# A Linformer attention and SwiGLU kernel: the second batch turned by DMA, k' turned over 128 rows, and the first batch's v' laid out by TensorE

## The chip, the cores and the metric

One core of a Trainium2 chip runs the whole program. The metric is the device time of one execution in microseconds. Before the change the median of 8 runs was 573.11 us (572.68 to 574.63).

A core has TensorE (matmuls, into PSUM), VectorE (DVE), ScalarE (ACT), GpSimd (POOL) and SyncE (SP), each with its own queue of instructions that runs in the order in which the program lists them; they wait for each other through semaphores. DMA transfers are issued from POOL (all loads that change float32 to bf16), from SP (stores and turns) and from ACT.

## The reference

There are 8 batches of 8 heads, 1024 tokens and 64 elements a head. E and F project the 1024 tokens of k and v to 64 rows, so that attention is over 64 columns. The result is the input of a gated feed-forward block.

```python
k_proj = np.einsum('ks,bhsd->bhkd', E, k)
v_proj = np.einsum('ks,bhsd->bhkd', F, v)
scores = scale * np.matmul(q, k_proj.transpose(0, 1, 3, 2))
attn = softmax(scores)                       # over 64 columns
x = np.matmul(attn, v_proj)                  # -> [8192, 512]
g = x @ w_gate                               # [8192, 1536]
out = (g * sigmoid(g) * (x @ w_val)) @ w_out # [8192, 512]
```

## The kernel before, in words

**Tiles.** A batch's 1024 tokens make two tiles of 512 (`ch` 0 and 1), so the feed-forward block runs over 16 tiles `c = 2 b + ch`. In each, 12 column blocks `f` of 128 are worked off. `f_g` makes four matmuls of 512 columns into a `gps` bank and has ACT take the tanh; `f_v` makes four into a `vps` bank and has DVE multiply twice, into `hT`. The product with `w_out` of the tile before (`f_y`, parts of four matmuls into a `yps` bank, three parts to one of the four output blocks) is dealt out between them; for the first tile it begins only at the fifth block of the second (`ypart`), and there a block carries one or two parts.

**The attention's units.** For each batch: `u_KV` projects k and v (matmuls with 64 stationary columns: k to PSUM rows 0 to 63, v to rows 64 to 127), copies k' to a tile `ks` of 64 rows and v' into the block-diagonal `BDV`. `u_KT` turns k' with four TensorE transposes, one a pair of heads, into a bf16 PSUM tile, and four DVE copies bring it into the block-diagonal `BD`. Queries must stand with their elements on the partitions: either `u_T` turns four 128x128 blocks of them on TensorE and copies them out of PSUM, or `u_TD` has one DMA on the SP queue turn the 512 tokens of a tile, from `qb` to `qTd`. `u_S` makes four score matmuls and the exponential on ACT, `u_R` sums and takes the reciprocal on DVE, `u_N` multiplies on POOL. The softmax weights must be turned again: `u_A` on TensorE with a copy, or `u_AD` by one DMA on SP. `u_PV` multiplies by v' and copies into `xT`, the feed-forward block's input. A tile has four units of T, S, R, N and A and four of PV. `BY_DMA` says which tiles take the DMA way: all of batches 1 to 7 but the first tile of batch 1.

**The order.** The schedule is written by hand (`manual_schedule`): each engine's queue has the order of the program's text. The feed-forward loop has 192 steps `t`, `t = 12 c + f`; slot `2t` comes after `f_g`, slot `2t + 1` after `f_v` and the step's `f_y` parts. `put(slot, unit, ...)` hangs an attention unit into a slot, `place(b)` does so for batch b. In a slot loads go first, the rest in the order of the `put` calls. So TensorE runs through `f_g`, a slot's units, `f_v`, `f_y`, a slot's units; a unit whose input isn't there stops all that follows.

**The start.** Ahead of the loop batch 0's first tile is worked off unit by unit. Its loads, then the weights in pairs of column blocks (`load_w_gv`), the second tile's queries, `wo` and batch 1's k are issued on POOL, in text order, mixed with the `u_N` there; `warm` gives TensorE matmuls on zeros. In the first two steps the tile's two halves of 256 tokens are made apart (`u_PV2`, `f_mm` with `i`). Batch 0's second tile hangs in slots 12 to 23, batch 1 in slots 30 to 69.

**Buffers that matter.** Three PSUM banks `pa` for the attention, two `gps`, two `vps`, one `yps`; four `qb`, two each of `kb`, `vb`, `qTd`, `AT`, `AAd` and `xT` of each half; three `ysb` for outputs.

Of the kernel before, what the change touches and what calls it, by code (L numbers as in the profile page):

```python
# [15 lines left out]
B = 8  # L16
H = 8
# [13 lines left out]
BY_DMA = [(b, ch) for b in range(1, B) for ch in range(CH)][1:]  # L31
# [3 lines left out]
def kernel(  # L35
# [39 lines left out]
    BDV = [const.tile([P, NPAIR, P], BF16, name=f"BDV{i}") for i in range(2)]  # L75
    ET = const.tile([P, NJ, KP], BF16, name="ET")
# [26 lines left out]
    def load_q(b, ch, js=(0, 4)):  # L103
        if js[0] == 0:
            qb[b, ch] = q_pool.tile([P, H, 4, D], BF16, name="qb", tag="qb")
        js = slice(*js)
        nc.gpsimd.dma_start(  # L107
            out=qb[b, ch][:, :, js, :].rearrange("p h j d -> p h (j d)"),
            in_=q[b].rearrange("h (p c j) d -> p c h j d", c=2, j=4)[:, ch, :, js, :].rearrange(
                "p h j d -> p h (j d)"  # L110
            ),
        )
# [26 lines left out]
    def u_KV(b, what="kv", hs=(0, H), at="a"):  # L139

        key = (b, what)
        if key not in kvp:
            kvp[key] = bank(at, [P, H, D], FP32, "kvp")
        t = kvp[key]
        h0, h1 = hs
        todo = [x for x in (("k", 0, ET, kb), ("v", 64, FT, vb)) if x[0] in what]
        for j in range(NJ):
            for _, lo, w, src in todo:
                nc.tensor.matmul(  # L149
                    out=t[lo : lo + 64, h0:h1].rearrange("p h d -> p (h d)"),  # L150
                    lhsT=w[:, j, :],
                    rhs=src[b][:, h0:h1, j, :],
                    start=(j == 0),
                    stop=(j == NJ - 1),
                )
        if "k" in what:
            if (b, "s") not in kvp:
                kvp[b, "s"] = aw.tile([KP, H, D], BF16, name="ks", tag="ks")
            nc.scalar.copy(out=kvp[b, "s"][:, h0:h1], in_=t[0:64, h0:h1])  # L159
        if "v" in what:  # L160
            tv = t[64:128].rearrange("p (a c) d -> p a c d", c=2)
            ps = slice(h0 // 2, h1 // 2)
            eng = nc.vector if b else nc.scalar
            copy(eng, BDV[b % 2][0:64, ps, 0:64], tv[:, ps, 0, :])
            copy(eng, BDV[b % 2][64:128, ps, 64:128], tv[:, ps, 1, :])
        if h1 == H:
            kvp.pop(key)

    def u_KT(b, at="a", prs=(0, NPAIR)):

        ks = kvp[b, "s"]
        t = bank(at, [P, NPAIR, KP], BF16, "kTp")
        for pr in range(*prs):
            nc.tensor.transpose(
                out=t[:, pr, :],
                in_=ks[:, 2 * pr : 2 * pr + 2, :].rearrange("p h d -> p (h d)"),
                identity=ident_bf[:KP, :KP],
# [132 lines left out]


# [80 lines left out]
    def place(b):  # L392
        s0 = 48 * (b - 1)
        if b == 1:
            put(30, u_TD, 1, 1)
            put(34, u_KV, 1, "k")
            put(36, u_KT, 1)
            put(40, u_KV, 1, "v")
            sa = (37, 38, 39, 40, 48, 50, 52, 54)
            tt = (35, 36, 37, 38)  # L400
            ta = (41, 42, 43, 44)
            put(57, u_AD, 1, 1)
            sp = (43, 44, 45, 46, 66, 67, 68, 69)
        else:
            put(s0, u_KV, b)
            put(s0 + 3, u_KT, b)
            o = 14 if b == 2 else 6
            put(s0 + (3 if b == 2 else -6), u_TD, b, 0)
            put(s0 + (5 if b == 2 else -4), u_TD, b, 1)
# [4 lines left out]
        for j in range(NJ):  # L414
            if (b, j // 4) not in BY_DMA:
                put(tt[j], u_T, b, j)
                put(ta[j], u_A, b, j)
# [10 lines left out]
    with tc.manual_schedule():  # L428
# [17 lines left out]
        for i in range(2):  # L446
            nc.vector.memset(BD[i][:], 0.0)
            nc.vector.memset(BDV[i][:], 0.0)

# [65 lines left out]
        u_R(0, 3)  # L515
        u_N(0, 3)
        u_KV(0, "v", (0, 4), at="y")
        warm(1)
        u_KV(0, "v", (4, 6), at="y")
        u_PV2(0, 0, 0, 0, act)  # L520
        u_A(0, 2, dve)
        u_KV(0, "v", (6, 8), at="y")
        u_A(0, 1, act)
        u_PV2(0, 0, 1, 0, act)
        u_A(0, 3, dve)
        u_PV2(0, 0, 0, 1, dve)
        load_w_gv(4, 6)
        load_q(0, 1)
        for f in (6, 8, 10):
            load_w_gv(f, f + 2)  # L530
        load_wo(0)
        load_wo(1)
        load_k(1)
        f_mm(0, 0, 0, 0)
        u_PV2(0, 0, 1, 1, act)
        f_mm(0, 0, 1, 0)
        f_mm(0, 1, 0, 0)
        f_mm(0, 1, 1, 0)

        for i, u in enumerate(range(4, 8)):  # L540
            put(12 + i, u_T, 0, u)
            put(14 + i, u_S, 0, u)
            put(15 + i, u_R, 0, u)
            put(15 + i, u_N, 0, u)
            put(19 + i, u_A, 0, u, nc.scalar)
        put(21, u_PV, 0, 1, 0)
        put(22, u_PV, 0, 1, 1)
        put(23, u_PV, 0, 1, 2)
        put(23, u_PV, 0, 1, 3)
        put(20, load_q, 1, 0)  # L550
# [4 lines left out]
        for b in range(2, B):  # L555
            s0 = 48 * (b - 1) - (12 if b == 2 else 24)
            put(s0, load_k, b)
            put(s0 + 2, load_v, b)
            put(s0 + 4, load_q, b, 0)
            put(s0 + 6, load_q, b, 1)  # L560
# [53 lines left out]
```

The softmax here doesn't subtract the row's maximum and nothing guards it: scores larger than these inputs give would overflow.

## Time and profile before

| | |
|---|---|
| median of 8 runs | 573.11 us |
| the profiled execution's own time | 573.3 us |
| its span | 571.5 us |
| TensorE busy | 564.8 us |
| VectorE, ScalarE, GpSimd busy | 336.7, 238.3, 109.3 us |
| read from HBM, written | 60.29 MB, 16.78 MB |

The span runs from the program's first instruction to its last. A line of the timeline gives start and length in us, engine, line of the program, operation, what is written from what, shapes and how many instructions were merged; in brackets, idle time ahead and what ended it. A matmul's length is from its issue to its last result, so successive ones overlap: what TensorE really spends on a group is the distance from its start to the next group's start. Some matmul records are missing.

### The profile page before, as it was taken

The page shows a single profiled execution, that of the slowest core. Times are in us where ns is not written, and L with a number is a line of the kernel's source. Part 1 is how long each engine was busy: PE and PEld are TensorE (multiplying, and loading weights), DVE is VectorE, ACT ScalarE, POOL GpSimd, SP SyncE. Part 2 cuts the span into 40 slices and gives each one's busy share as a digit, 9 for nine tenths or more (in the row PEclk, how much of TensorE's full clock was granted, in tenths as well). Part 3 has the DMA queues.
Part 4 walks back from the last instruction along what each step waited for, and adds up shares of the span by engine and source line. Part 5 has one row for each costly group of instructions (what it writes and reads, how often), then busy time and mean ns, then how long its engine had stood idle before and what let it go on. Part 6 is the DMA issues. An engine that isn't in the chain of part 4 may idle for free.

```text
span 571.5 us, 7944 instructions
## 1 busy us (share of the span) xinstructions
PE 564.8 (99%) x2971; PEld 268.7 (47%) x2971; DVE 336.7 (59%) x581; ACT 238.3 (42%) x421; POOL 109.3 (19%) x122
## 2 busy tenths in 40 slices
PE   8999999999999999999999999999999999999997
PEld 4654444444444444444444444444444444444444
DVE  3777566666466654666556664567546674554540
ACT  3555534354435434444335434354342543443232
POOL 6734122134002500124001330023200220000000
PEclk9999999999999999999999999999999999999999
DMA  9999993549901697038950499204990123100012
GB/s 209 171 200 206 202 174 79 87 74 195 203 27 48 114 192 145 19 75 131 189 106 37 65 174 193 67 20 93 194 175 36 44 50 75 38 37 24 33 38 92
DMA packets 106983, 61.86 MB, mean 108 GB/s; under 512 B 60096, under 2 KB 98240, under 8 KB 106944
## 3 DMA queue, kind: packets, MB, share of 16 engines
q0 software_dynamic: 42800, 29.36, 35.7%
q1 hardware_dynamic: 63232, 30.42, 24.8%
q10 hardware_dynamic: 912, 1.57, 0.9%
q8 instruction: 23, 0.38, 0.3%
q14 instruction: 16, 0.13, 0.1%
HBM read 60.29 MB, written 16.78 MB: 135 GB/s over the span
## 4 chain that ended last, share of the span: by engine, by line
PE 92%; DMA 3%; POOL 1%; DVE 1%; ACT 1%; issue 0%; DVEq 0%; POOLq 0%
PE yps L362 29%; PE vps L324 28%; PE gps L324 27%; PE kvp L149 3%; PE sc L229 2%; PE pv L287 2%; DMA wv<-in_moe_w_val_dram 2%; DMA kb<-in_k_dram 2%; DVE zz L244 1%; POOL wg L117 0%; DVE hT L348 0%; ACT xT L137 0%; POOL qb L107 0%; DVE s L343 0%; POOL AA L260 0%
## 5 line engine op out<-in xcount | busy, mean ns | idle before, releaser
L343 DVE SCALAR_TENSOR_TENSOR s<-th,gps 128x512 f32<-128x512 f32 x192 | 130.6, 680 | 139.1 <-ACT th L336 138.7
L324 PE MATMUL gps<-xT,wg 128*128 128x512 bf16 (+1 forms) x776 | 197.8, 377 | 0.6 <-DMA wg<-in_moe_w_gate_dram 0.4
L324 PE MATMUL vps<-xT,wv 128*128 128x512 bf16 (+1 forms) x776 | 197.5, 377 | 0.1
L362 PE MATMUL yps<-wo,hT 128*128 128x512 bf16 (+1 forms) x780 | 194.5, 376 | 0.0
L336 ACT ACTIVATE th<-gps 128x512 f32<-128x512 f32 x192 | 114.6, 597 | 163.4 <-PE gps L324 161.9
L348 DVE TENSOR_TENSOR hT<-s,vps 128x512 bf16<-128x512 f32 x192 | 132.0, 688 | 22.1 <-PE vps L324 1.5
L362 PEld LDWEIGHTS <-hT 128*128 128x128 bf16 x780 | 76.1, 98 | 89.9
L260 POOL TENSOR_TENSOR AAd<-ee,rr 128x512 bf16<-128x512 f32 x52 | 54.1, 1040 | 319.5 <-issue 178.1
L324 PEld LDWEIGHTS <-wv 128*128 128x128 bf16 x776 | 73.8, 98 | 83.1 <-issue 3.3
L324 PEld LDWEIGHTS <-wg 128*128 128x128 bf16 x776 | 74.0, 98 | 81.8 <-DMA wg<-in_moe_w_gate_dram 0.9
L372 ACT ACTIVATE ysb<-yps 128x512 f32<-128x512 f32 (+1 forms) x65 | 38.4, 590 | 78.1 <-PE yps L362 78.1
L137 ACT CAST xT<-pv 128x512 bf16<-128x512 f32 x63 | 36.7, 584 | 51.2 <-PE pv L287 50.3
L244 DVE TENSOR_REDUCE zz<-ee 128x8 f32<-128x512 f32 x64 | 43.4, 679 | 19.4 <-ACT ee L233 19.3
L233 ACT ACTIVATE ee<-sc 128x512 f32<-128x512 f32 x64 | 37.9, 596 | 17.8 <-PE sc L229 17.7
L287 PE MATMUL pv<-AT,BDV 128*128 128x512 bf16 x60 | 22.6, 379 | 0.0
L229 PEld LDWEIGHTS <-qTd 128*128 128x128 bf16 x208 | 16.0, 98 | 12.3
L229 PE MATMUL sc<-BD,qTd 128*128 128x128 bf16 x208 | 20.1, 219 | 0.0
L137 DVE CAST BDV<-kvp 64x256 bf16<-64x256 f32 x14 | 6.0, 427 | 22.1 <-ACT ks L159 19.1
L260 POOL TENSOR_TENSOR AA<-ee,rr 128x512 bf16<-128x512 f32 x11 | 11.4, 1038 | 36.3 <-DVE rr L246 34.4
L246 DVE RECIPROCAL rr<-zz 128x8 f32<-128x8 f32 x64 | 13.0, 203 | 6.7 <-DVE zz L244 0.5
L149 PE MATMUL kvp<-kb,ET 128*64 128x512 bf16 (+1 forms) x72 | 15.5, 357 | 0.6 <-DMA kb<-in_k_dram 0.4
L149 PE MATMUL kvp<-vb,FT 128*64 128x512 bf16 (+2 forms) x80 | 15.6, 338 | 0.3 <-ACT BDV L137 0.3
(51 smaller groups left out, 147.4 us busy)
## 6 DMA issues: line engine op xcount, KB each, us to landing
out_dram<-ysb SPq DMA_DIRECT2D x63, 256.0 KB, 2.4
qb<-in_q_dram POOLq DMA_DIRECT2D x15, 512.0 KB, 16.8
kb<-in_k_dram POOLq DMA_DIRECT2D x7, 1024.0 KB, 11.3
vb<-in_v_dram POOLq DMA_DIRECT2D x7, 1024.0 KB, 14.4
wo<-in_moe_w_out_dram POOLq DMA_DIRECT2D x2, 768.0 KB, 15.3
wg<-in_moe_w_gate_dram POOLq DMA_DIRECT2D x5, 256.0 KB, 9.6
wv<-in_moe_w_val_dram POOLq DMA_DIRECT2D x5, 256.0 KB, 10.2
kraw<-in_k_dram ACTq DMA_DIRECT2D x2, 512.0 KB, 5.1
```

The lines of the kernel that those rows point to most:

```text
L137: (nc.scalar.copy if eng is nc.scalar else eng.tensor_copy)(out=out, in_=in_)
L149: nc.tensor.matmul(out=t[lo : lo + 64, h0:h1].rearrange("p h d -> p (h d)"), lhsT=w[:, j, :], rhs=src[b][:, h0:h1, j, :], start=(j == 0), ...
L229: nc.tensor.matmul(out=ps[:, n, :], lhsT=t[:, n, :], rhs=BD[b % 2][:, 4 * g + n, :], start=True, stop=True)
L233: nc.scalar.activation(out=e[:].rearrange("p h j k -> p (h j k)"), in_=ps[:].rearrange("p a k -> p (a k)"), func=AF.Exp, scale=scale,)
L244: nc.vector.reduce_sum(out=z[:], in_=e[:], axis=AX.X)
L260: eng.tensor_tensor(out=a.rearrange("p j h k -> p h j k"), in0=ee.pop((b, u))[:], in1=rr.pop((b, u))[:].unsqueeze(3).to_broadcast([P, 4, 2 ...
L324: nc.tensor.matmul(out=ps[:, ts], lhsT=(wg, wv)[w][:, kt, f * P : (f + 1) * P], rhs=x[:, kt, ts], start=(kt == 0), stop=(kt == NKT - 1),)
L336: nc.scalar.activation(out=th[:], in_=ps[:], func=AF.Tanh, scale=0.5)
L343: nc.vector.scalar_tensor_tensor(out=s1[:], in0=th[:], scalar=1.0, in1=g[:], op0=ALU.add, op1=ALU.mult)
L348: nc.vector.tensor_tensor(out=hT[c][:, f, :], in0=s1[:], in1=ps[:], op=ALU.mult)
L362: nc.tensor.matmul(out=yy[c][:, cs], lhsT=hT[c][:, f, i * P : (i + 1) * P], rhs=wo[:, f, cs], start=(f == 0), stop=(f == NFT - 1),)
L372: nc.scalar.activation(out=ysb[:, cs], in_=yy[c][:, cs], func=AF.Copy, scale=0.5)
```

## The change

- `BY_DMA` takes in batch 1's first tile: its `u_T` and `u_A` are gone, a `u_TD` (slot 22) and a `u_AD` (slot 41) come. Batch 1's other units move: k in slot 29, k' turned in 32, scores in 35 to 38 and 41 to 44, `u_AD` of the second tile in 47.
- k' is kept in two constant tiles `ks` of 128 rows whose lower half is zero, and `u_KT` uses ordinary matmuls over all 128 rows into a float32 PSUM tile.
- Batch 0's v' is made by a new `u_V0` that writes the block-diagonal form in PSUM (a matmul on zeros first, then v in two column halves), so that one copy on ACT brings it to `BDV`. It is split over pairs 0 and 1, pair 2, pair 3, with a new `u_PV1` for one pair; the units around it and the first `f_mm` are put in another order.
- Loads: the queries of batch 0's second tile in two halves by heads, between the weights; batch 1's first queries and k ahead of `wo`; batch 2's k, v and queries in slots 43 to 45 (before, in 36 to 42), batch 3's four slots later than before.
- Batch 0's second tile moves one slot ahead, its `u_A` to 17, 18, 20, 21, its `u_PV` to 19, 20, 22, 22, the last with its copy on DVE. In batch 2 k and v are projected in slot 56 (before 48), k' turned in 59, `u_TD` in 57 and 59, and the scores start in 61 (before 62).

```diff
...
 NIT = B * CH * NFT
-BY_DMA = [(b, ch) for b in range(1, B) for ch in range(CH)][1:]
+BY_DMA = [(b, ch) for b in range(1, B) for ch in range(CH)]
 @with_exitstack
...
     BDV = [const.tile([P, NPAIR, P], BF16, name=f"BDV{i}") for i in range(2)]
+    ks = [const.tile([P, H, D], BF16, name=f"ks{i}") for i in range(2)]
     ET = const.tile([P, NJ, KP], BF16, name="ET")
...
             )
-    def load_q(b, ch, js=(0, 4)):
-        if js[0] == 0:
+    def load_q(b, ch, js=(0, 4), hs=(0, H)):
+        if js[0] == 0 and hs[0] == 0:
             qb[b, ch] = q_pool.tile([P, H, 4, D], BF16, name="qb", tag="qb")
-        js = slice(*js)
+        js, hs = slice(*js), slice(*hs)
         nc.gpsimd.dma_start(
-            out=qb[b, ch][:, :, js, :].rearrange("p h j d -> p h (j d)"),
-            in_=q[b].rearrange("h (p c j) d -> p c h j d", c=2, j=4)[:, ch, :, js, :].rearrange(
+            out=qb[b, ch][:, hs, js, :].rearrange("p h j d -> p h (j d)"),
+            in_=q[b, hs].rearrange("h (p c j) d -> p c h j d", c=2, j=4)[:, ch, :, js, :].rearrange(
                 "p h j d -> p h (j d)"
...
         if "k" in what:
-            if (b, "s") not in kvp:
-                kvp[b, "s"] = aw.tile([KP, H, D], BF16, name="ks", tag="ks")
-            nc.scalar.copy(out=kvp[b, "s"][:, h0:h1], in_=t[0:64, h0:h1])
+            nc.scalar.copy(out=ks[b % 2][0:64, h0:h1], in_=t[0:64, h0:h1])
         if "v" in what:
...
             ps = slice(h0 // 2, h1 // 2)
-            eng = nc.vector if b else nc.scalar
-            copy(eng, BDV[b % 2][0:64, ps, 0:64], tv[:, ps, 0, :])
-            copy(eng, BDV[b % 2][64:128, ps, 64:128], tv[:, ps, 1, :])
+            nc.vector.tensor_copy(out=BDV[b % 2][0:64, ps, 0:64], in_=tv[:, ps, 0, :])
+            nc.vector.tensor_copy(out=BDV[b % 2][64:128, ps, 64:128], in_=tv[:, ps, 1, :])
         if h1 == H:
             kvp.pop(key)
+    def u_V0(p0, p1, at):
+        t = bank(at, [P, p1 - p0, P], FP32, "kvp")
+        nc.tensor.matmul(
+            out=t[:].rearrange("p a d -> p (a d)"),
+            lhsT=zeros[:, 0:P], rhs=zeros[:, 0 : (p1 - p0) * P],
+            start=True, stop=False,
+        )
+        src = vb[0][:].rearrange("p (a c) j d -> p a c j d", c=2)
+        for j in range(NJ):
+            for c in range(2):
+                nc.tensor.matmul(
+                    out=t[64 * c : 64 * c + 64, :, 64 * c : 64 * c + 64],
+                    lhsT=FT[:, j, :],
+                    rhs=src[:, p0:p1, c, j, :],
+                    start=False,
+                    stop=(j == NJ - 1),
+                )
+        nc.scalar.copy(out=BDV[0][:, p0:p1, :], in_=t[:])
     def u_KT(b, at="a", prs=(0, NPAIR)):
-        ks = kvp[b, "s"]
-        t = bank(at, [P, NPAIR, KP], BF16, "kTp")
+        t = bank(at, [P, NPAIR, KP], FP32, "kTp")
         for pr in range(*prs):
-            nc.tensor.transpose(
+            nc.tensor.matmul(
                 out=t[:, pr, :],
-                in_=ks[:, 2 * pr : 2 * pr + 2, :].rearrange("p h d -> p (h d)"),
-                identity=ident_bf[:KP, :KP],
+                lhsT=ks[b % 2][:, 2 * pr : 2 * pr + 2, :].rearrange("p h d -> p (h d)"),
+                rhs=ident_bf[:, 0:KP],
+                start=True,
+                stop=True,
             )
...
         copy(eng, xT[b, ch][:, 2 * g : 2 * g + 2, 256 * i : 256 * (i + 1)], ps[:])
+    def u_PV1(b, ch, pr, i, eng):
+        ps = ps_a.tile([P, CW // 2], FP32, name="pv", tag="pa")
+        nc.tensor.matmul(
+            out=ps[:].rearrange("p (j t) -> p j t", t=P),
+            lhsT=BDV[b % 2][:, pr, :],
+            rhs=AT[b, ch][:, 2 * i : 2 * i + 2, pr, :],
+            start=True,
+            stop=True,
+        )
+        copy(eng, xT[b, ch][:, pr, 256 * i : 256 * (i + 1)], ps[:])
     gp = {}
...
         if b == 1:
+            put(22, u_TD, 1, 0)
+            put(29, u_KV, 1, "k")
+            put(32, u_KT, 1)
+            put(40, u_KV, 1, "v")
+            sa = (35, 36, 37, 38, 41, 42, 43, 44)
+            put(41, u_AD, 1, 0)
             put(30, u_TD, 1, 1)
-            put(34, u_KV, 1, "k")
-            put(36, u_KT, 1)
-            put(40, u_KV, 1, "v")
-            sa = (37, 38, 39, 40, 48, 50, 52, 54)
-            tt = (35, 36, 37, 38)
-            ta = (41, 42, 43, 44)
-            put(57, u_AD, 1, 1)
-            sp = (43, 44, 45, 46, 66, 67, 68, 69)
+            put(47, u_AD, 1, 1)
+            sp = (44, 45, 46, 46, 66, 67, 68, 69)
         else:
-            put(s0, u_KV, b)
-            put(s0 + 3, u_KT, b)
-            o = 14 if b == 2 else 6
-            put(s0 + (3 if b == 2 else -6), u_TD, b, 0)
-            put(s0 + (5 if b == 2 else -4), u_TD, b, 1)
+            put(s0 + (8 if b == 2 else 0), u_KV, b)
+            put(s0 + (11 if b == 2 else 3), u_KT, b)
+            o = 13 if b == 2 else 6
+            put(s0 + (9 if b == 2 else -6), u_TD, b, 0)
+            put(s0 + (11 if b == 2 else -4), u_TD, b, 1)
             sa = [s0 + o + 3 * j for j in range(NJ)]
...
         for j in range(NJ):
-            if (b, j // 4) not in BY_DMA:
-                put(tt[j], u_T, b, j)
-                put(ta[j], u_A, b, j)
             put(sa[j], u_S, b, j)
...
         for i in range(2):
+            nc.vector.memset(ks[i][64:P], 0.0)
             nc.vector.memset(BD[i][:], 0.0)
-            nc.vector.memset(BDV[i][:], 0.0)
+        nc.vector.memset(BDV[1][:], 0.0)
         def turn(which, at, halves=(0, 1)):
...
         u_R(0, 3)
+        u_V0(0, 2, "y")
+        u_PV2(0, 0, 0, 0, act)
+        warm(1)
+        u_V0(2, 3, "y")
+        u_A(0, 2, dve)
+        u_PV1(0, 0, 2, 0, dve)
+        u_V0(3, 4, "v")
+        u_PV1(0, 0, 3, 0, act)
         u_N(0, 3)
-        u_KV(0, "v", (0, 4), at="y")
-        warm(1)
-        u_KV(0, "v", (4, 6), at="y")
-        u_PV2(0, 0, 0, 0, act)
-        u_A(0, 2, dve)
-        u_KV(0, "v", (6, 8), at="y")
+        f_mm(0, 0, 0, 0)
         u_A(0, 1, act)
-        u_PV2(0, 0, 1, 0, act)
         u_A(0, 3, dve)
-        u_PV2(0, 0, 0, 1, dve)
+        f_mm(0, 0, 1, 0)
+        u_PV2(0, 0, 0, 1, act)
+        u_PV2(0, 0, 1, 1, dve)
+        f_mm(0, 1, 0, 0)
+        f_mm(0, 1, 1, 0)
         load_w_gv(4, 6)
-        load_q(0, 1)
-        for f in (6, 8, 10):
-            load_w_gv(f, f + 2)
+        load_q(0, 1, hs=(0, 4))
+        load_w_gv(6, 8)
+        load_q(0, 1, hs=(4, 8))
+        load_w_gv(8, 10)
+        load_w_gv(10, 12)
+        load_q(1, 0)
+        load_k(1)
         load_wo(0)
         load_wo(1)
-        load_k(1)
-        f_mm(0, 0, 0, 0)
-        u_PV2(0, 0, 1, 1, act)
-        f_mm(0, 0, 1, 0)
-        f_mm(0, 1, 0, 0)
-        f_mm(0, 1, 1, 0)
         for i, u in enumerate(range(4, 8)):
-            put(12 + i, u_T, 0, u)
-            put(14 + i, u_S, 0, u)
-            put(15 + i, u_R, 0, u)
-            put(15 + i, u_N, 0, u)
-            put(19 + i, u_A, 0, u, nc.scalar)
-        put(21, u_PV, 0, 1, 0)
-        put(22, u_PV, 0, 1, 1)
-        put(23, u_PV, 0, 1, 2)
-        put(23, u_PV, 0, 1, 3)
-        put(20, load_q, 1, 0)
+            put(11 + i, u_T, 0, u)
+            put(13 + i, u_S, 0, u)
+            put(14 + i, u_R, 0, u)
+            put(14 + i, u_N, 0, u)
+            put((17, 18, 20, 21)[i], u_A, 0, u, nc.scalar)
+        put(19, u_PV, 0, 1, 0)
+        put(20, u_PV, 0, 1, 1)
+        put(22, u_PV, 0, 1, 2)
+        put(22, u_PV, 0, 1, 3, nc.vector)
         put(20, load_v, 1)
...
         for b in range(2, B):
-            s0 = 48 * (b - 1) - (12 if b == 2 else 24)
-            put(s0, load_k, b)
-            put(s0 + 2, load_v, b)
-            put(s0 + 4, load_q, b, 0)
-            put(s0 + 6, load_q, b, 1)
+            s0 = 48 * (b - 1) - (20 if b == 3 else 24)
+            at = (43, 43, 44, 45) if b == 2 else (s0, s0 + 2, s0 + 4, s0 + 6)
+            put(at[0], load_k, b)
+            put(at[1], load_v, b)
+            put(at[2], load_q, b, 0)
+            put(at[3], load_q, b, 1)
         for s in slots:
             slots[s].sort(key=lambda x: x[0] not in (load_k, load_v, load_q))
```

## The prediction

> **What bounds the kernel now.** I read the page's busy times first, then the chain that ended last.
>
> ```profile
> PE 564.8 (99%) x2971; PEld 268.7 (47%) x2971; DVE 336.7 (59%) x581; ACT 238.3 (42%) x421; POOL 109.3 (19%) x122
> ...
> PE 92%; DMA 3%; POOL 1%; DVE 1%; ACT 1%; issue 0%; DVEq 0%; POOLq 0%
> ```
>
> TensorE is busy for 564.8 of 571.5 us and carries 92% of the chain; the DMA share of it is the weights' landing before 34 us. A busy TensorE isn't proof, so I looked at starts: four 512-column matmuls follow each other every 0.863 us through the whole body. So from about 34 us on, time moves one for one with (a) what TensorE is given and (b) how often it stands. The places where it stands are few. Its timeline at the weights:
>
> ```profile
> 31.18 1.03 PE L324 MATMUL vps<-xT,wv 128*128 128x512 bf16 x4
> 32.59 1.04 PE L324 MATMUL gps<-xT,wg 128*128 128x512 bf16 x4 [0.38 <-DMA wg<-in_moe_w_gate_dram]
> 33.46 0.39 PE L195 MATMUL qTp<-ident_bf,qb 128*128 128x128 bf16 x4
> ```
>
> 31.18 + 0.863 = 32.04, but the next starts at 32.59: 0.54 lost to the gate weights; after the four transposes (33.46 + 0.22) the value weights cost another 0.27 (the next starts at 33.96). At the change of tile:
>
> ```profile
> 42.88 1.03 PE L324 MATMUL vps<-xT,wv 128*128 128x512 bf16 x4
> 43.90 0.40 PE L276 MATMUL aTp<-ident_bf,AA 128*128 128x128 bf16 x4
> ...
> 46.97 1.48 PE L324 MATMUL gps<-xT,wg 128*128 128x512 bf16 x4
> 48.29 1.02 PE L324 MATMUL vps<-xT,wv 128*128 128x512 bf16 x4
> ```
>
> 1.32 instead of 0.863 from 46.97 (it waits for xT copies), and 1.02 at 42.88: 0.46 + 0.15 lost. At k':
>
> ```profile
> 62.55 1.03 PE L324 MATMUL gps<-xT,wg 128*128 128x512 bf16 x4
> ...
> 63.51 0.29 PE L174 MATMUL kTp<-ident_bf,ks 64*128 64x64 bf16 x4
> 63.73 0.40 PE L195 MATMUL qTp<-ident_bf,qb 128*128 128x128 bf16 x4
> 63.96 1.03 PE L324 MATMUL vps<-xT,wv 128*128 128x512 bf16 x4
> ```
>
> A gps group starts at 62.55, so it is through at 63.41; the four 64-row kTp start at 63.51 and the next group at 63.73. The kTp themselves are 0.033 apart: about 0.10 is lost going in and 0.09 coming out. The same two gaps stand at every later k'. The four transposes take 0.22.
>
> Then the DMA issues, alone in their windows: the turn and the loads.
>
> ```profile
> 63.41 6.99 SPq L207 DMA_TRANSPOSE qTd<-qb  x1
> ...
> 87.54 2.35 SPq L207 DMA_TRANSPOSE qTd<-qb  x1
> ...
> 102.50 1.32 SPq L214 DMA_TRANSPOSE AT<-AAd  x1
> ```
>
> The first one, beside loads, lands 13.1 us after its issue, the other two 4.4 and 4.3 us after.
>
> **What the Trainium skill says.** TensorEngine Tiling (Array Packing), Tiling Modes: "Changing tiling mode (not just tile) drains the TensorE". The trace agrees: 0.10 and 0.09 us around 64-row kTp, 0.09 around 64-column kvp, none between 128x128 forms. TensorE: Matmul & The Clock Gate, Back-to-back issue gap: N/2.4 + 2.5 ns, so 56 and 216 ns; the trace has 0.223/4 and 0.863/4. The same page, Part 1, says that an idle stretch can put TensorE back to half clock for a window of 3.4 us; the trace shows half speed only at the very start (the first warm matmuls start 0.43 us apart, later ones 0.22). DMA: Bandwidth & Descriptors, Issuing engines are not separate DMA queues: transfers of all queues interleave on the same 16 engines. The trace agrees: 1 MB loads end 5.2 to 5.6 us apart, but v of batch 2, beside the turn, 6.8 us after k (issued 47.46 and 48.32, 21.2 and 27.2 us to landing).
>
> **The change, part by part.**
>
> 1. Batch 1's first half turned by DMA: 4 query and 4 weight units leave TensorE: 8 x 0.223 = **-1.79**. The copies that leave (4 x 0.58 ACT, 4 x 0.41 DVE) were hidden and give nothing. Added: two SP transposes.
>
> 2. k' over 128 rows: the drains go. Seven batches lie in the saturated part: 7 x 0.19 = **-1.33**. The matmul may cost more or less than 0.033 as a plain 128-row one; taken as equal, bounds 0 and +0.03 x 28 = +0.8 (the transposes' 0.056 as ceiling). Its output is f32, so the four DVE copies to BD cost not 0.28 but up to 0.43 each (the BDV row of the same shape): +0.6 us a batch, covered by DVE's 41% idle time. Tightest is batch 2: turn in slot 59, scores in 61, that is one gps, vps and yps group later, 2.6 us; copies end after about 0.3 + 4 x 0.43 = 2.0. Without that cover 0 to 0.5.
>
> 3. q of tile 1 in two halves, the second behind weights 6 and 7. Those weights land 1.3 us earlier (256 KB ahead of them less): **-0.81**. The first half (heads 0 to 3) serves the first two query turns, the second lands near 34 and is wanted in slot 13, near 34.7.
>
> 4. Tile 1's units one to three slots sooner, last xT copy on DVE: the 0.61 go; but the first u_PV (slot 19) now follows the u_A whose copy it needs (slot 18) by one 0.86 us group, and ACT has tanh (0.60) and then that copy (0.58) in between: it stands about 0.35. **-0.26**; bounds -0.61 and +0.3.
>
> 5. Start, first batch's v' in u_V0. Column halves run as pairs (in the full kvp the kb and vb matmuls start together, 16 in 1.85 us), so u_V0 is cheaper on TensorE than the three kvp groups; one ACT copy replaces two. But pair 3 is queued behind u_PV1 of pair 2, which waits for the AT copy on DVE: near 19.5. Then u_V0 0.6, BDV copy 0.3, u_PV1, xT copy 0.4, with 0.1 to 0.2 of semaphore at each: xT of pair 3 near 21.3, against 21.15 for the last input of the first gps before, and two u_A units (0.45) now come after it. k' in f32 adds 0.1 to 0.2 to the first scores. I take **+0.3** at the first full gps (25.14 before); bounds -0.3 and +0.9.
>
> Sum: -1.79 - 1.33 - 0.81 - 0.26 + 0.30 = **-3.9 us**. The profiled run took 573.3 (span 571.5, 1.8 around it): 569.4, and 0.2 less against the median of 573.1: **569.2**.
>
> 6. What hides the rest. *Loads.* wo goes behind q(1,0) and k(1). k(1) landed at 52.4 (32.82 + 19.6) behind 1.5 MB of wo; now behind 0.5 MB: 5.1 sooner, 47.3, and about 48 beside the early turn, which SP issues as soon as q(1,0) lands near 42.5. It is wanted in slot 29, where a gps of 52.60 stood, shifted by -0.8: 51.8, so 3.8 to spare. wo's second half goes from 47.4 to 47.4 + 7.6 + 2.7 for the turn's 512 KB = 57.7; wanted by the third matmul of the second yps, near 60.4. If late, it stops TensorE and, through yps, ACT's copy and tanh behind it. q(1,1) 63.4 + 2.7 = 66.1; its turn, now with no load beside it, 4.4: 70.5; wanted in slot 41, near 73. Queued behind that turn on SP are the first outputs, as before (70.45 before, about 68.5 now), with three ysb.
> *The turned weights.* The fourth unit's scores are two slots earlier, near 66; before, from scores (73.06) to the end of POOL's product (79.0) took 5.9, so 70 to 72; plus 4.3: 74.3 to 76.3. Wanted by u_PV in slot 44, near 78.3. Batch 2's loads on POOL follow the fifth product (about 75.5), so they don't run beside it; they delay the sixth by 1.8, which nobody awaits until slot 66. k(2), v(2) land near 82.5 and 88, wanted in slot 56 near 95.
> *Batch 2's later turns* were nearly late: AT issued at 125.59 landed 17.8 later, at 143.4, for a pv at 143.90. Now it is one slot sooner and k(3) four later: safer.
>
> **Rivals.**
> - *One transfer or copy is late by 1 to 2.5 us* (wo, the turned weights, or the start's upper bounds together). For it: margins of 2 to 4 us on a DMA system that is full until 66 us. Against: every margin was taken with the turn's full bytes. 570.2 to 572.2.
> - *TensorE falls back to half clock in the looser start.* For it: waits near 17, 19 and 20.5 between short groups. Against: the page's clock row has 9 throughout, and one warm matmul stays. 3.4 us at half: +1.7 to +3.4, 571 to 572.6.
> - *Slower: k(1) stops TensorE in slot 29.* It decides from landing at 55.7 (51.8 + 3.9); slower by 0.2% from 56.8. If POOL's loads stood still while the early turn is in flight (13.1), k(1) would land at 60.4: +8.6 - 3.9, about 578. Against: beside the turn of before 1 MB still took only 6.8 instead of 5.2 to 5.6.
> - *It doesn't do what it says*: if k' as a full matmul still drains, 1.3 less gain, 570.5.
>
> **How the numbers follow.** My forecast 0.70 (its own range 567.9 to 570.4, from the bounds of parts 2, 4 and 5 partly cancelling), late transfer 0.12, half clock 0.06, drains stay 0.04, slower 0.08. 0.2% is 1.15 us, about what a measurement can tell here: faster below 571.96, slower above 574.26. Nearly all of the first case and most of the next three are faster: 0.84; same 0.07, slower 0.09. Range 567.8 to 572.3 leaves out the slower case and the tails.
>
> **What would show it.** kTp as 128*128 with no gap around it; no wait for wg near 32; 32 qTp and 32 aTp (8 units fewer in all); first full gps between 24.8 and 26; kvp of k(1) near 51.8 without a DMA wait; wo, qTd and AT waits of TensorE all absent from its list of waits; body from 100 us on identical in rhythm but for kTp. Wrong if TensorE waits for kb, wo, AT or qTd near 52, 60, 73 or 78, or if the first gps comes later than 26.

## The result, and the profile after

The changed kernel takes 569.96 us (569.77 to 570.76); the kernel before took 573.21 us (572.67 to 575.22) beside it. The ratio is 0.9942 with an interval of 0.9934 to 0.9950. The profiled execution took 569.97 us with a span of 568.2.

The busy times and the chain of the changed kernel, from its page:

```profile
PE 559.7 (99%) x2966; PEld 266.2 (47%) x2966; DVE 340.3 (60%) x580; ACT 235.6 (41%) x413; POOL 109.8 (19%) x123
...
PE 95%; DMA 3%; ACT 1%; POOL 1%; DVE 0%; issue 0%; POOLq 0%
```

TensorE has 5.1 us less to do and still carries the chain. Now its timeline at the places where the prediction saw it stand. At the weights:

```profile
31.45 1.03 PE L358 MATMUL vps<-xT,wv 128*128 128x512 bf16 x4
32.32 0.39 PE L217 MATMUL qTp<-ident_bf,qb 128*128 128x128 bf16 x4
32.54 1.03 PE L358 MATMUL gps<-xT,wg 128*128 128x512 bf16 x4
```

31.45 + 0.863 gives 32.32 (rounded), and 0.22 later the gate matmuls begin: both stops (0.54 and 0.27) are gone. At the change of tile:

```profile
40.59 1.03 PE L358 MATMUL vps<-xT,wv 128*128 128x512 bf16 x4
41.70 0.38 PE L309 MATMUL pv<-AT,BDV 128*128 128x512 bf16 x1
...
46.45 1.03 PE L358 MATMUL gps<-xT,wg 128*128 128x512 bf16 x4
47.32 1.03 PE L358 MATMUL vps<-xT,wv 128*128 128x512 bf16 x4
```

The gate group of the new tile takes its plain 0.87 (1.32 before), and the first `u_PV` stands 0.25 (41.70 less 41.45) for the copy of its weights. At batch 1's k':

```profile
55.31 1.03 PE L358 MATMUL gps<-xT,wg 128*128 128x512 bf16 x4
56.17 0.28 PE L194 MATMUL kTp<-ident_bf,ks 128*128 128x64 bf16 x4
56.29 1.03 PE L358 MATMUL vps<-xT,wv 128*128 128x512 bf16 x4
```

The four kTp begin when the gate group is through and the next group begins 0.12 later: nothing is lost on either side. Before, 0.32 lay between the gate group's end (63.41) and the next group (63.73), so this is worth 0.20. From 160 us on TensorE's work differs in nothing but these turns, and there five of them carry TensorE's lead from 2.65 to 3.70 us: 0.21 each. One wait is new. It stands in no line of before and in no line of the sum:

```profile
103.54 1.03 PE L396 MATMUL yps<-wo,hT 128*128 128x512 bf16 x4
104.92 0.40 PE L251 MATMUL sc<-BD,qTd 128*128 128x128 bf16 x4 [0.35 <-DMA qTd<-qb]
```

The scores in slot 61 could begin at 103.54 + 0.863 = 104.40 and begin at 104.92: batch 2's first turned queries are 0.52 late. From 30 us on this is the only wait for a DMA in TensorE's list of waits. Behind it: the page's row of before for loads of k, and the DMA issues of the changed kernel at the time of batch 2's loads (size, us from issue to landing).

```profile
kb<-in_k_dram POOLq DMA_DIRECT2D x7, 1024.0 KB, 11.3
```

```profile
kb<-in_k_dram POOLq DMA_DIRECT2D x1, 1024.0 KB, 10.8
vb<-in_v_dram POOLq DMA_DIRECT2D x1, 1024.0 KB, 16.7
```

k(2), issued at 76.17, lands at 86.95, v(2) at 93.84, q(2,0) at 98.10; SP issues the turn at 98.15, and it lands 6.7 us later, at 104.87. Batch 1's second turn, with no load beside it, landed 4.3 us after its issue (66.36 to 70.63); this one ran beside batch 2's second queries, which landed at 103.20. With the 4.3 of the other it would have been there near 102.5, ahead of the 104.40 (an estimate from these two turns).

At the end, the last store as ACT issues it, first before, then after:

```profile
568.86 0.36 ACTq L374 DMA_DIRECT2D out_dram<-ysb  x1
```

```profile
565.16 0.36 ACTq L408 DMA_DIRECT2D out_dram<-ysb  x1
```

568.86 to the span's end at 571.53 is 2.7 us, 565.16 to 568.19 is 3.0. By the trace's events both stores land 1.68 us after the issue begins; from that landing to the end 0.98 passed before and 1.34 after.

The tally, by the start of the last TensorE matmul (568.22 before, 564.52 after, so -3.70):

| step | us |
|---|---|
| eight turning units gone | -1.79 |
| k' without drains, 7 x 0.21 | -1.47 |
| weights' waits gone | -0.81 |
| change of tile, -0.61 + 0.25 | -0.36 |
| start (first full gps 25.14, now 25.41) | +0.27 |
| new wait for the turned queries of batch 2 | +0.52 |
| sum | -3.64 |

0.06 stays unexplained; it lies before 49 us, where the changed kernel is 0.97 ahead and the rows above give 0.90. Then comes +0.36 at the end, and the span is shorter by 3.3.

### The profile page after: what moved, and what is told of

Its sections match the earlier page's. It is cut to its first block, busy times and chain, and to the rows that moved or that the text cites. A ratio compares the mean times of both kernels' runs of the same rounds, so it can differ in the third digit from the quotient of the medians.

```text
span 568.2 us, 7931 instructions
## 1 busy us (share of the span) xinstructions
PE 559.7 (99%) x2966; PEld 266.2 (47%) x2966; DVE 340.3 (60%) x580; ACT 235.6 (41%) x413; POOL 109.8 (19%) x123
## 4 chain that ended last, share of the span: by engine, by line
PE 95%; DMA 3%; ACT 1%; POOL 1%; DVE 0%; issue 0%; POOLq 0%
PE gps L358 29%; PE yps L396 29%; PE vps L358 29%; PE kvp L150 3%; PE sc L251 2%; PE pv L309 2%; DMA kb<-in_k_dram 2%; DMA qTd<-qb 1%; PE aTp L298 0%; ACT ee L255 0%; ACT th L370 0%; PE qTp L217 0%; POOL AA L282 0%; POOL qb L108 0%; PE pv L324 0%
## 5 line engine op out<-in xcount | busy, mean ns | idle before, releaser
L282 POOL TENSOR_TENSOR AAd<-ee,rr 128x512 bf16<-128x512 f32 x56 | 58.3, 1043 | 342.9 <-issue 156.4
L138 ACT CAST xT<-pv 128x512 bf16<-128x512 f32 (+1 forms) x62 | 35.9, 582 | 51.8 <-PE pv L309 50.5
L251 PE MATMUL sc<-BD,qTd 128*128 128x128 bf16 x224 | 21.7, 219 | 0.4 <-DMA qTd<-qb 0.4
L108 POOL DMA_DIRECT2D qb<-in_q_dram x18 | 16.3, 906 | 0.6 <-DMA qb<-in_q_dram 0.6
L150 PE MATMUL kvp<-kb,ET 128*64 128x512 bf16 (+1 forms) x72 | 15.5, 358 | 0.1
L162 DVE CAST BDV<-kvp 64x256 bf16<-64x256 f32 x7 | 3.0, 426 | 19.9 <-ACT ks L158 17.8
L150 PE MATMUL kvp<-vb,FT 128*64 128x512 bf16 x56 | 13.4, 382 | 0.0
```

The lines of the kernel that those rows point to most:

```text
L138: (nc.scalar.copy if eng is nc.scalar else eng.tensor_copy)(out=out, in_=in_)
L150: nc.tensor.matmul(out=t[lo : lo + 64, h0:h1].rearrange("p h d -> p (h d)"), lhsT=w[:, j, :], rhs=src[b][:, h0:h1, j, :], start=(j == 0), ...
L251: nc.tensor.matmul(out=ps[:, n, :], lhsT=t[:, n, :], rhs=BD[b % 2][:, 4 * g + n, :], start=True, stop=True)
L282: eng.tensor_tensor(out=a.rearrange("p j h k -> p h j k"), in0=ee.pop((b, u))[:], in1=rr.pop((b, u))[:].unsqueeze(3).to_broadcast([P, 4, 2 ...
```

## Experiments

None of the kernels below leaves out any computation. Each is compared with the kernel before on the same chip, whose median was 572.87 to 572.98 us there. The changed kernel itself ran again only beside the last of them; elsewhere the ratios and the timelines are compared. Unless another base is named, the edit is made to the changed kernel.

### k' back to 64-row transposes

```diff
-        t = bank(at, [P, NPAIR, KP], FP32, "kTp")
+        t = bank(at, [P, NPAIR, KP], BF16, "kTp")
-            nc.tensor.matmul(
-                lhsT=ks[b % 2][:, 2 * pr : 2 * pr + 2, :]...,
-                rhs=ident_bf[:, 0:KP], start=True, stop=True)
+            nc.tensor.transpose(
+                in_=ks[b % 2][0:64, 2 * pr : 2 * pr + 2, :]...,
+                identity=ident_bf[:KP, :KP])
```

> The changed kernel with k' turned as before, by 64-row transposes into bf16, the rest as changed. Theory (each k' turn in the saturated part drains TensorE twice, 0.20 us in all): seven turns, +1.4 us, so 571.4, and gaps of 0.10 and 0.09 us around kTp again. Rival (the drains lie in time that TensorE would stand anyway): 570.0, within 0.3.

571.01 us, ratio 0.9967 (0.9955 to 0.9979). TensorE's timeline at the same k':

```profile
55.19 1.03 PE L356 MATMUL gps<-xT,wg 128*128 128x512 bf16 x4
56.15 0.29 PE L194 MATMUL kTp<-ident_bf,ks 64*128 64x64 bf16 x4
56.37 1.04 PE L356 MATMUL vps<-xT,wv 128*128 128x512 bf16 x4
```

The gate group is through at 56.05; 0.10 is lost before the kTp, and the next group begins 0.32 after the gate group's end (56.37) instead of 0.12: 0.20 a batch. The last matmul comes 1.03 later than in the changed kernel, although the start was 0.12 quicker here and the new wait only 0.20 instead of 0.52. With these put back the drains are worth 1.03 + 0.12 + 0.32 = 1.47 over seven batches, as in the tally. The drains are real, and the 128-row form does away with them.

### That edit alone, on the kernel before

```diff
+    ks = [const.tile([P, H, D], BF16, name=f"ks{i}") for i in range(2)]
...
-            nc.tensor.transpose(
+            nc.tensor.matmul(
```

> The kernel before with one part of the change alone: k' kept in two tiles of 128 rows with a zero lower half, turned by full matmuls into f32. Theory (seven turns in the saturated part, two drains of 0.10 each): -1.4 on TensorE's last matmul and -1.2 to -1.5 in time, 571.5 to 571.7. Rival (the f32 copies to BD come late and TensorE waits for them): less than -0.8.

571.59 us, ratio 0.9978 (0.9968 to 0.9988). The last matmul comes 1.68 sooner. The first full gps comes 0.33 sooner, but the weights take part of that back, and at 50 us, before the first of the seven turns, 0.20 of it is left: 1.48 for the drains. From both sides the edit is worth 1.47 to 1.48; the prediction had 1.33. It changes three things at once: the rows, the operation (transpose or matmul) and the type in PSUM. The query turns `qTp` tell them apart. They are transposes into a bf16 PSUM tile too, but over 128 rows, and nothing is lost around them (32.32 and 32.54 in the lines of the result). So the operation and the type aren't the cause, and the row count is left.

### Batch 1's first tile turned by TensorE again

```diff
-BY_DMA = [(b, ch) for b in range(1, B) for ch in range(CH)]
+BY_DMA = [(b, ch) for b in range(1, B) for ch in range(CH)][1:]
-            put(22, u_TD, 1, 0)
-            put(41, u_AD, 1, 0)
+            tt = (33, 34, 35, 36)
+            ta = (39, 40, 41, 42)
+            if (b, j // 4) not in BY_DMA:
+                put(tt[j], u_T, b, j)
+                put(ta[j], u_A, b, j)
```

> The changed kernel with the first tile of batch 1 turned by TensorE again (four units each of queries and weights, in slots 33 to 36 and 39 to 42) and its two turns on SP gone. Theory (TensorE's time counts one for one): 8 x 0.223 = +1.79 on TensorE's last matmul. Two stores-queue transfers fewer also put the last store's semaphore back to the second-last place in SP's closing list, so about 0.36 less after the last store: +1.4 in all, 571.4. Rival (the closing list plays no part): +1.8, 571.8. Rival (the turn by DMA only exchanged TensorE work for waits): 570.0.

571.33 us, ratio 0.9974 (0.9964 to 0.9984). The last matmul is at 566.36, 1.84 later. The start cost 0.38 more here, and the stop at slot 61 is 0.20 instead of 0.52, so the eight units are worth 1.84 - 0.38 + 0.32 = 1.78, where 8 x 0.223 is 1.79. The other half of the question was the end of the program: with two transfers fewer, the last store's landing to the end is 0.98 again, as in the kernel before. In time, what TensorE lost comes back by 0.36.

### More transfers, to turn the order at the end

A trace's events show what lies in that 0.36. SP ends the program by waiting for the eight semaphores of its and ACT's transfers, always in the same order and at about 0.06 us each. Transfers take the semaphores in rotation, so the number of transfers decides which one the last store has: in the kernel before it stood last but one in SP's order, in the changed kernel first, with seven more waits after it (six more, 6 x 0.06 = 0.36). Seven further transfers should put it near the end again:

```diff
+        parts = [slice(0, 256), slice(256, DM)] if 8 <= c < 15 and i == 1 else [cs]
+        for cs in parts:
             eng.dma_start(
```

> The changed kernel with seven of its stores in the middle cut in two halves, so that seven more transfers are issued from SP and the last store falls on the last of the eight semaphores that SP waits for at the end. Theory (what is left of the end after the last landing is one wait of 0.06 for each semaphore that stands behind the last store's in SP's closing list: seven in the changed kernel, one before): last landing to end from 1.34 to about 0.92, -0.4: 569.5. Rival (the 0.36 longer end of the profile is chance): 570.0, end 1.34 or scattered.

569.80 us, ratio 0.9949 (0.9937 to 0.9962). ACT's issue of the last store:

```profile
565.10 0.36 ACTq L410 DMA_DIRECT2D out_dram<-ysb  x1
```

From there to the end at 567.70 it is 2.6 us, and landing to end 0.91: the last store's semaphore is now the last in SP's order. So the number of transfers does set the length of the end. But the time outside the span is 1.8 to 2.0 us in this kernel's executions (2.0 in the profiled one) and 1.7 to 1.9 in the others, and the ratio is no better than the changed kernel's 0.9942 and 0.9953: the span's gain isn't seen in the time. Why is open.

### The second tile's queries whole, ahead of the weights

```diff
-        load_q(0, 1, hs=(0, 4))
+        load_q(0, 1)
         load_w_gv(6, 8)
-        load_q(0, 1, hs=(4, 8))
```

> The changed kernel with the second tile's queries of batch 0 loaded in one piece, ahead of weights 6 and 7, as before. Theory (the wait of 0.54 + 0.27 before 34 us was the weights' order alone): +0.5 to +0.8, 570.5 to 570.8, with a wait of gps for wg near 33. Rival (the weights come in time now, since the first full gps starts 0.3 later): +0.2 or less.

570.20 us (569.45 to 571.58), ratio 0.9955 (0.9944 to 0.9967). The profiled execution:

```profile
33.62 0.39 PE L217 MATMUL qTp<-ident_bf,qb 128*128 128x128 bf16 x4
34.84 1.04 PE L358 MATMUL vps<-xT,wv 128*128 128x512 bf16 x4 [0.83 <-DMA wv<-in_moe_w_val_dram]
```

33.62 + 0.22 = 33.84, so 1.0 is lost to the value weights, with 0.2 more for the gate weights: the wait that the split removed is back, and with 1.2 larger than the 0.81 before. This profile is of the slowest of six executions. The median lies only 0.24 above the changed kernel's first one, and the scatter is two us wide. That would fit weights and TensorE that race here, with a loser that changes from one execution to the next, but the other executions have no profile. Where the cause stands is shown; its size in the median isn't.

### Batch 2's loads in their old slots

```diff
-            at = (43, 43, 44, 45) if b == 2 else (s0, s0 + 2, s0 + 4, s0 + 6)
+            at = (36, 38, 40, 42) if b == 2 else (s0, s0 + 2, s0 + 4, s0 + 6)
```

> The changed kernel with batch 2's loads in slots 36, 38, 40, 42 as before, so that POOL issues k and v while batch 1's first weights are still to be turned. Theory (the turn needs the queues empty): AT of the first tile takes 8 to 17 us from issue to landing instead of 5.6, TensorE stands 3 to 8 us at pv in slot 44, and the 0.5 us wait for qTd near 104 goes: 572.5 to 577. Rival (the turn has margin enough, 2.2 us): 569.5, the 0.5 us gained.

589.83 us, ratio 1.0301 (1.0284 to 1.0317). TensorE's waits from 30 us on (in total, times, longest), then its timeline:

```profile
PE sc L251 <- DMA qTd<-qb: 10.8, 1, 10.8
PE pv L309 <- DMA AT<-AAd: 4.7, 1, 4.7
```

```profile
84.09 0.61 PE L251 MATMUL sc<-BD,qTd 128*128 128x128 bf16 x4 [10.85 <-DMA qTd<-qb]
84.49 1.91 PE L358 MATMUL gps<-xT,wg 128*128 128x512 bf16 x4
86.20 0.63 PE L251 MATMUL sc<-BD,qTd 128*128 128x128 bf16 x4
```

Nothing on POOL holds k(2) back now: it is issued at 45.12, right behind batch 1's second queries, and v(2) and the queries of batch 2 follow from 67.29 on. So batch 1's second turn (issued 67.06) runs beside the rest of k(2), which lands at 72.31, and beside v(2). It needs 17.0 us to landing instead of 4.3, and the turned weights 20.4 instead of 5.6. This is more than the 3 to 8 us that I gave it: I had the first wait at the turned weights, but the queries were late before them. And a second cost was in nobody's sum: after the stall the four gate matmuls take 86.20 - 84.49 = 1.71 instead of 0.863. TensorE runs at half speed for 3.5 us after the first stall (84.09 to 87.62) and for 5.4 after the second (95.90 to 101.27), which loses half of that, about 4.4 us. (The prediction's rival had counted on 3.4 us at half speed; the second stretch was longer.) So stalls of 15.5 us cost 20. "TensorE falls back to half clock", a rival of the prediction for the start, exists; here it followed two stalls of 10.85 and 4.7 us, and the stops of 0.2 to 1.0 us seen elsewhere were not followed by half speed.

It follows that moving these loads behind the fifth product is what the DMA turn of batch 1 rests on, with 2.2 us to spare at slot 44 (landed 75.96, read at 78.16), and that the same move is what makes batch 2's first turn late. Against the old slots it buys 20 us, and it gives back half a microsecond.

### Batch 2's scores one slot later again

```diff
-            o = 13 if b == 2 else 6
+            o = 14 if b == 2 else 6
```

> The changed kernel with batch 2's scores, products and turns of weights one slot later (first scores in 62 as before, no longer in 61). Theory (TensorE stood 0.52 for the turned queries of batch 2 because their load landed near 98 and slot 61 asks at 104.4): the wait goes, since slot 62 asks 0.86 later: -0.5 against the changed kernel, about 569.4. Rival (the wait only moves to a later turn or to pv): 570.0.

569.66 us (569.36 to 570.35), ratio 0.9943 (0.9930 to 0.9955). The wait for the turned queries is gone from TensorE's list, and no later one has come in its place. The time doesn't show it beyond the scatter. The profile is of the slowest of the five executions (570.35): its first full gps came at 25.93, 0.52 later than in the changed kernel, and near 35 us TensorE stood 0.35 for the second half of the second tile's queries. The last matmul (564.87) is 0.35 later than there, so of these 0.87 the missing wait gave back its 0.52.

### The first batch's v' as before, and pair 3 ahead of the first pair-2 product

The prediction put the start's +0.3 down to pair 3, queued behind a `u_PV1` that waits for DVE. TensorE's timeline of the changed kernel there:

```profile
17.25 0.39 PE L324 MATMUL pv<-AT,BDV 128*128 128x256 bf16 x2 [0.47 <-ACT BDV L185]
19.13 0.27 PE L336 MATMUL pv<-AT,BDV 128*128 128x256 bf16 x1 [0.52 <-DVE AT L138]
20.19 0.28 PE L336 MATMUL pv<-AT,BDV 128*128 128x256 bf16 x1 [0.36 <-ACT BDV L185]
```

Pair 3's product (20.19) waits for a copy that can begin only after `u_V0(3, 4)`, which stands behind the wait at 19.13. Two kernels tell the unit from its place. One takes the whole v' part back:

```diff
-        u_V0(0, 2, "y")
...
-        u_V0(3, 4, "v")
-        u_PV1(0, 0, 3, 0, act)
+        u_KV(0, "v", (0, 4), at="y")
+        u_KV(0, "v", (4, 6), at="y")
+        u_PV2(0, 0, 0, 0, act)
+        u_KV(0, "v", (6, 8), at="y")
+        u_PV2(0, 0, 1, 0, act)
...
```

> The changed kernel with batch 0's v' made as before (three kvp groups, two ACT copies each, the old order of units and first gps around them). Theory (u_V0 with its order costs about 0.3 at the start, as its pair 3 waits behind u_PV1 of pair 2): first full gps near 25.0 instead of 25.41, -0.2 to -0.4: 569.7. Rival (u_V0 gains what its fewer copies save and the 0.27 comes from k' in f32 and the later scores): the first full gps later than 25.41, +0.2 to +0.6, 570.2 to 570.6.

The other only swaps two lines:

```diff
+        u_V0(3, 4, "v")
         u_PV1(0, 0, 2, 0, dve)
-        u_V0(3, 4, "v")
```

> The changed kernel with u_V0 of pair 3 ahead of u_PV1 of pair 2, which waits 0.69 for the AT copy on DVE. Theory (pair 3 is late because it stands behind that wait): its BDV copy comes 0.5 sooner, the waits of 0.53 at its u_PV1 and 0.30 in the first gps shrink, first full gps near 24.9, -0.4 to -0.5: 569.5. Rival (the next inputs, the AT copies of the first tile's second half, are late anyway): -0.1 or nothing.

The old v': 569.27 us (569.21 to 569.36), ratio 0.9935 (0.9921 to 0.9948). Pair 3 first: 569.83 us (569.36 to 570.17), ratio 0.9943 (0.9930 to 0.9955). With pair 3 first the two products follow each other without a stop between them, so that the timeline merges them:

```profile
19.15 0.56 PE L336 MATMUL pv<-AT,BDV 128*128 128x256 bf16 x2
19.55 0.89 PE L358 MATMUL gps<-xT,wg 128*128 128x256 bf16 x4
24.65 1.02 PE L358 MATMUL gps<-xT,wg 128*128 128x512 bf16 x3
```

The start varies with the landing of the first transfers, so I compare it from the last score matmul of the first tile to the first full gps. That stretch is 9.53 in the changed kernel (and 9.52 or 9.53 in the seven other profiles with this start), 9.20 in the kernel before, 9.12 with the old v', 8.74 with pair 3 first. So `u_V0` isn't dearer than what it replaced; its order was. Put right, it beats the old start by 0.4. TensorE then reaches the second tile's queries earlier and stands there (0.24 at 33.9) for the second half of them. The last matmul comes 0.61 sooner than in the changed kernel: a start quicker by 0.76, less 0.25 at the queries, and 0.10 less at slot 61. The profile is of the quickest of the five executions, and the median shows little of it. The old v' gains 0.68 in its profile, but only 0.18 of that at the start; 0.50 is the stop at slot 61, which is 0.02 there.

That stop isn't made by a quicker start. In the six profiles with these slots and units (the changed kernel twice, whole queries, more transfers, old v', pair 3 first) TensorE could begin the scores of slot 61 28.23 us after POOL issued k(2), since both follow TensorE's own progress. From that issue to the landing of the turned queries it took 28.20 us with the old v' and 28.57 to 29.08 in the five others. The stop, 0.02 to 0.90, is what the transfers need beyond that, within 0.05; why they need more or less is open. Slot 62 gives them 29.09.

### All repairs of the schedule together, with the changed kernel beside them

```diff
-            o = 13 if b == 2 else 6
+            o = 14 if b == 2 else 6
+        u_V0(3, 4, "v")
         u_PV1(0, 0, 2, 0, dve)
-        u_V0(3, 4, "v")
-        put(19, u_PV, 0, 1, 0)
+        put(20, u_PV, 0, 1, 0)
```

> The changed kernel with three repairs: pair 3 of u_V0 ahead of the waiting u_PV1, batch 2's scores from slot 62, the first u_PV of tile 1 in slot 20 and not 19. Theory (each wait is worth what it showed: 0.24 at pv, 0.4 to 0.5 at qTd, 0 to 0.5 at the start): -0.7 to -1.2 against the changed kernel on the same chip, 568.7 to 569.2. Rival (the start's gain is taken back by the weights, which land no sooner): -0.6, 569.3.

The same with the old v' in the place of the swap:

```diff
-            o = 13 if b == 2 else 6
+            o = 14 if b == 2 else 6
-        put(19, u_PV, 0, 1, 0)
+        put(20, u_PV, 0, 1, 0)
```

> The changed kernel with batch 0's v' made as before, batch 2's scores from slot 62 and the first u_PV of tile 1 in slot 20. Theory (the 0.24 at pv goes; the wait for qTd was absent from the one profile with v' as before, so slot 62 adds nothing there): -0.2 against the kernel with v' as before alone, -0.6 to -0.9 against the changed one: 569.0. Rival (u_PV one slot later makes the first gps of tile 1 wait): 569.4.

And the changed kernel without any edit:

> The changed kernel itself, once more, beside the others on the same chip. Every theory: 569.8 to 570.1. If the 0.52 at qTd near 104 and the 0.36 in the closing list are fixed properties, a second profile shows both; if the start varies by itself, the first full gps moves between 25.0 and 26.0.

On one chip: all repairs 569.01 us (568.95 to 569.25), ratio 0.9932 (0.9920 to 0.9945); old v' with the rest 569.18 us (569.12 to 569.37), 0.9935 (0.9922 to 0.9947); the changed kernel 570.48 us (569.44 to 570.71), 0.9953 (0.9939 to 0.9966). In the first, TensorE's list has no wait for a DMA after 30 us; what is left is 0.14 at 34.2 and 0.19 at the last two `u_PV` (44.8). Those didn't stand in the changed kernel, so moving the first `u_PV` gained not its 0.25 but some 0.05. The last matmul comes at 563.64 instead of 565.02. The version with all repairs has the lowest time and ratio of the study and is quicker by 1.5 us than the changed kernel beside it; the two intervals overlap by a little (0.9939 to 0.9945), but the ranges of their executions don't. The two repaired versions can't be told apart.

The changed kernel again gives 0.9953 where it gave 0.9942 at first, and its executions scatter by 1.3 us, those of the repaired ones by 0.3. Its second profile (570.48) shows where 0.50 of that comes from, by which its last matmul is later than in the first (564.52): the start is the same within 0.02, but the second half of the second tile's queries landed at 35.02 instead of 33.63, for which TensorE stood 0.33, and the stop at slot 61 was 0.66 instead of 0.52. The closing 1.34 us were there again (1.36). So two transfers land close to the time they are wanted, at 34 and at 104 us; for the executions without a profile it isn't shown.

## Why the prediction was right, step by step

It said 569.2, within 567.8 to 572.3, and faster; 569.96 came. In terms of the profiled execution, 569.4 was worked out and 569.97 measured. That the sum came so near is in part luck: two costs that it did not list (0.88 together) met gains that were larger than forecast by some 0.3, and the same kernel's second median was 570.48.

- **Part 1, the turn.** 8 x 0.223 = 1.79 stood up: undone, it moves the last matmul by 1.78, start and slot 61 set apart. The transfers added weren't free, though: they cost 0.36 at the end, which the part put at nothing.
- **Part 2, k'.** 0.19 a batch was 0.20 to 0.21; the equal price of the new matmuls holds (0.029 apart). The dearer copies to BD, 0.41 to 0.43, are hidden as said: at slot 61 the last one ended at 103.94, and the scores could begin at 104.40.
- **Part 3, the queries in halves.** Both stops gone, -0.81, and back with the split undone. The second half was said to land near 34 and to be wanted near 34.7. It landed at 33.63 and at 35.02 in the two profiles of the changed kernel, and in four profiles of the study TensorE stood 0.15 to 0.35 there.
- **Part 4, the change of tile.** The wait at slot 19 was taken at 0.35 and was 0.25, so -0.36 instead of -0.26. This rests on the timelines: no kernel takes back this part alone.
- **Part 5, the start.** The order was rightly named: it makes the stretch behind the last scores 0.33 longer, and swapping the two lines takes that away. That the first full gps then came at +0.27 is partly chance, as the scores themselves came 0.06 sooner, and their place moves by 0.7 among the profiles.
- **Part 6, what hides the rest.** This is where a term was missing. The step "k(2), v(2) land near 82.5 and 88" took the spacing of loads in a full stream, 5.2 to 5.6 us a megabyte. The queue was empty here, and the row for single loads of k, 11.3 us from issue to landing, stood on the page: k(2) landed at 86.95, v(2) at 93.84. Both were still early for slot 56, but the chain behind them, the queries of batch 2, their turn and the scores of slot 61, was never listed, and these came 0.52 late. With it two of the prediction's signs did not hold: no wait for qTd in TensorE's list, and the same rhythm from 100 us on. Of the others, k(1) landed at 47.43 (said about 48), the second half of wo at 58.08 (57.7), the second queries at 66.3 (66.1), their turn at 70.6 (70.5), the turned weights at 75.96 (74.3 to 76.3); none stopped TensorE. The early turn, issued at 41.80 beside the loads, needed 18.8 us and landed at 60.6 for scores at 61.47: it got no time of its own in the prediction and had only 0.9 to spare.

So the sum's error of +0.55 (-3.89 worked out, -3.34 in the span) is 0.52 for the new wait and 0.36 for the end, less 0.10 at part 4, 0.14 at k', 0.03 at the start and the unexplained 0.06. A late transfer was a rival at 1 to 2.5 us; it came, in another place and at a fifth to a half of that, beside the forecast gains and not instead of them. Half clock at the start and a stop for k(1) did not come.

## What to carry to other kernels

Follow each moved load to its last reader, through the turn that waits for it, and time its landing by the issue-to-landing row of a load under the same conditions, an idle queue or a full one, not by the spacing of a stream. The DMA turns here were quick (4.3 us) only when no load ran beside them, so a change that replaces TensorE's turns by DMA stands or falls with where the loads go. In a kernel bound by TensorE a stop that is taken away lets it reach sooner the transfers that were issued long before, as the second tile's queries here; a transfer whose issue follows TensorE's progress, as k(2) here, moves along with it. So repair the waits of the first kind together, and judge them together.

## What the runs showed that I had not expected

- A DMA turn of 512 KB landed 4.3 us after its issue with no load beside it, 6.7 beside the end of one and 17.0 beside batch 2's loads; the turned weights 5.6 with only stores beside them, and 20.4 beside those loads.
- After a stall of 10.85 us, and again after one of 4.7, TensorE ran at half speed, for 3.5 and for 5.4 us.
- The end of the program depends on the number of transfers before it: 0.91 to 1.36 us from the last store's landing to the last instruction, at about 0.06 us for every semaphore that is waited for behind it.
- A 1 MB load issued into an idle queue (k(2)) took 10.8 us, twice the 5.2 us by which such loads follow each other in a stream. Its first packet moved 1.65 us after the issue, and until it landed the queue moved 1.34 MB: part of v(2), issued 0.94 later, had gone with it. How the rest of the time is made up isn't shown.
